# A state-space convolution kernel: the last unit's rows read back step by step, and the last quarter's output made in two halves of 64 channels

## The chip, the cores and the metric

The kernel runs on one core of a Trainium2 chip. A core has a matrix engine (TensorE, in the profile PE, with its weight loads as PEld), VectorE (DVE), ScalarE (ACT), GpSimd (POOL) and SyncE (SP), and sixteen DMA engines that move data between DRAM and the on-chip memory SBUF. TensorE writes its results into another on-chip memory, PSUM. Every engine works through its own list of instructions in order and waits on semaphores. The metric is the time of one execution on the device in microseconds (us), as the median of several runs.

## What is computed

Two diagonal state-space layers (S4 and S4D) are applied to one sequence of 2048 steps and 512 channels. Each is a long causal convolution along the sequence, written with FFTs in the reference, and a gate from a dot product with the input mixes the two results:

```python
def reference(A_u, ..., gate_w):
    x = A_u
    g = _sigmoid((x * gate_w).sum(-1, keepdims=True))
    a = _A_ref(x, ...)   # K = Re sum_n C * exp(dt*A*l) * dt*B;  y = irfft(rfft(u)*rfft(K)) + u*Dskip
    b = _B_ref(x, ...)   # K = 2 Re sum_n C*dt * exp(dt*A*l);    y = irfft(rfft(u)*rfft(K)) + u*D_skip
    return g * a + (1 - g) * b
```

All data are 32-bit floats.

## The kernel before

The 512 channels are worked in eight units of 64, `v` = 0 to 7; two units make a quarter `q` = `v // 2`, which is also the unit of output. For each unit GpSimd, ScalarE, VectorE and TensorE first make the two convolution filters ("tables", `chunk`), TensorE does a first transform stage (`put`), and then `stage2` runs eight steps, `mg` = 0 to 7, over four frequencies each: a forward transform on TensorE (`forward`, line 719), a product with the spectrum `U` of the input on VectorE (lines 791 and 794), an inverse transform on TensorE (lines 803 and 804) into a PSUM bank `hb`, a copy on ScalarE into one of two SBUF buffers `st` (line 807), and a store of 256 KB into the DRAM scratch `wt` (line 810). The spectra `U` are read back from DRAM scratch (line 782); they were stored there earlier in pairs of 128 and 64 partitions (lines 758 to 766).

The last transform needs the data turned: what lay along partitions has to lie in rows. That is what the trip through `wt` is for. `final(q)` reads both units of a quarter back (line 825) and works on four banks `bk`: for each bank two loads of 512 KB, one of unit 2q and one of unit 2q+1, each over 128 partitions, then 16 matmuls with 128 moving columns (64 channels of each unit, line 836) with the weights `wb` and `wg`, which hold the gate, one copy of the bank (line 845 or 847) and one store of 256 KB to the output (line 848). In the last quarter the four banks' rows go into the SBUF buffers `F`, `AB`, `AB` and `Fp` (the last one is a part of the tile `X`, and stands as X in the profile).

The order of all work is made ahead of time, in Python, by a list scheduler (`Plan.run`). Every operation has an engine, an assumed cost, a due time and dependencies. At each point of the modelled time each engine takes, among the operations that are ready and find a free buffer, the one with the lowest due time. DMAs are issued on SyncE's queue; there the model adds 1.1 us and the bytes at 360 GB/s on a single wire, and what depends on a DMA becomes ready 1.2 us after its modelled end. The order that results is emitted as it is: on each engine, SyncE's queue too, an instruction that waits holds up all behind it.

`FILL` names places in TensorE's order (counted in operations) at which spare matmuls of an identity matrix go in (line 300), whose results nobody reads. Place 304 is the first operation of the last quarter's `final`; there 29 units stand ahead of it.

Of the kernel before, what the change touches and what calls it, by code (L numbers as in the profile page):

```python
# [13 lines left out]
P = 128  # L14
L = 2048
D = 512
NJ, NS = 32, 64
NV = 8
EV = (58, 57, 196, 105, 4, 199, 64, 66)
EU = (15, 96, 247, 5)  # L20
NQ = 4
NCH = 128
NCK = 16
CHUNKS = ((1, 0), (1, 1), (0, 0), (0, 1), (1, 2), (1, 3), (0, 2), (0, 3))
LAST = ("Fp", "AB", "AB", "F")
ZU = (95, 116, 87, 62)
GE = 0
OE = (7, 10, 2, 0)
# [34 lines left out]
FPRE = 4.308  # L63
# [11 lines left out]
FW = -2.217  # L75


FILL = {1: 2, 3: 7, 5: 14, 17: 3, 49: 8, 50: 2, 51: 5, 54: 2, 55: 1, 88: 2, 160: 29, 161: 14, 162: 5, 199: 10, 201: 12, 213: 1, 275: 6, 304: 29, 22: 3, 32: 2, 33: 1, 52: 1, 53: 1, 57: 1, 58: 3, 66: 1, 68: 1, 71: 1, 181: 1, 189: 3, 196: 1, 198: 9, 200: 2, 202: 3, 244: 1, 249: 1}


def _flat(t):
# [27 lines left out]
class Plan:  # L109
# [44 lines left out]
    def run(self):  # L154
        free = {t: [(0.0, i) for i in range(len(l))] for t, l in self.tiles.items()}
        caps = {c: [0.0] * n for c, n in CAPS.items()}
        at = dict.fromkeys(("T", "A", "V", "G", "D"), 0.0)
        wire, lanes = 0.0, [0.0] * 8
        table = "E"
        ready = {e: [] for e in at}  # L160
        for o in self.ops:
            o.wait, o.succ = len(o.deps), []
        for o in self.ops:
            for d in o.deps:
                d.succ.append(o)
            if not o.wait:
                ready[o.eng].append((0.0, o))
        n, now, order, turn = 0, 0.0, [], 0
        while n < len(self.ops):
            nxt = 1e30  # L170
            for e in at:
                if at[e] > now:
                    nxt = min(nxt, at[e])
                    continue
                best = None
                for k, (rt, o) in enumerate(ready[e]):
                    if rt > now:
                        nxt = min(nxt, rt)
                        continue
                    key = o.due + (SWITCH if o.func and o.func != table else 0.0)  # L180
                    if best is not None and key >= best[0]:
                        continue
                    need, ok = {}, True
                    for b in o.bufs:
                        if b.slot is None and b.tag:
                            need[b.tag] = need.get(b.tag, 0) + 1
                            if b.cls:
                                need[b.cls] = need.get(b.cls, 0) + 1
                    for t, m in need.items():
                        l = sorted(caps[t]) if t in caps else sorted(f for f, _ in free[t])  # L190
                        if len(l) < m or l[m - 1] > now:
                            ok = False
                            if len(l) >= m:
                                nxt = min(nxt, l[m - 1])
                    if e == "D" and lanes[0] > now:
                        ok = False
                        nxt = min(nxt, lanes[0])
                    if ok:
                        best = (key, k, o)
                if best is None:  # L200
                    continue
                o = best[2]
                ready[e].pop(best[1])
                if e == "T":
                    if turn in FILL:
                        order.append(self.spare(FILL[turn], min((f, t, i) for t in ("ps", "sd") for f, i in free[t])))
                    turn += 1
                cost = o.cost
                if o.func and o.func != table:
                    table, cost = o.func, cost + 1.3  # L210
                at[e] = now + cost
                o.start, o.end = now, now + cost
                if e == "D":
                    wire = max(wire, now + cost + 0.6) + o.nbytes / 360e3
                    o.end = wire
                    lanes = sorted(lanes[1:] + [o.end])
                nxt = min(nxt, at[e])
                for b in o.bufs:
                    if b.slot is None and b.tag:
                        l = free[b.tag]  # L220
                        i = min(range(len(l)), key=lambda j: l[j])
                        b.slot = l.pop(i)[1]
                        b.t = self.tiles[b.tag][b.slot]
                        if b.cls:
                            caps[b.cls].remove(min(caps[b.cls]))
# [20 lines left out]
def gated_s4_mix(ctx: ExitStack, tc: tile.TileContext, ins: dict, out: bass.AP):  # L246
    nc = tc.nc
    V, G, A, T = nc.vector, nc.gpsimd, nc.scalar, nc.tensor
    DMA = nc.sync.dma_start
# [3 lines left out]
    ps = ctx.enter_context(tc.tile_pool(name="ps", bufs=1, space=bass.MemoryType.PSUM))  # L253
    dr = ctx.enter_context(tc.tile_pool(name="dr", bufs=1, space=bass.MemoryType.DRAM))
    pl = Plan()
    op = pl.op
# [9 lines left out]
    wt_t = dr.tile([NV, NJ, P, P], F32, tag="wt", name="wt")  # L266
# [4 lines left out]
    def bank(cls="fb"):  # L271
        return Buf("ps", cls)
# [495 lines left out]
    def both(a):  # L768

        return bass.AP(a.tensor, a.offset, [[512, P], [64 * 512, 2], [1, 512]])  # L770

    def stage2(v, due, sp):
        F, q = Ft[v], v // 2
        fw = [done[v, 0, 0]]
        for mg in range(8):
# [22 lines left out]
            def mms(mg=mg, Z1=Z1, Z2=Z2, hb=hb):  # L798
# [5 lines left out]
                    T.matmul(o, Tw[:, m, 64:192], zv(Z2), start=False, stop=True)  # L804

            op("T", 1.79, dm, mms, r=[Z1, Z2, TwB], w=[hb])
            op("A", 0.48, dm, lambda hb=hb, st=st: A.copy(st.t, hb.t), r=[hb], w=[st])  # L807
            op(
                "D", 0.5, dm,
# [2 lines left out]
                ),  # L812
                r=[st], w=[(wt[v], ((mg, mg + 1),))], nbytes=262144,
            )

    def final(q, due):

        for bk in range(4):
            dy = due + YSP[q] * bk / 4
            f, y, o = Buf(LAST[bk] if q == NQ - 1 else "Fp"), bank(), Buf("st")  # L820
            fv = lambda f=f: f.v("p (u s k c) -> p u s k c", u=2, s=8, k=2, c=64)
            for u in range(2):
                op(
                    "D", 0.5, dy - FPRE,
                    lambda f=f, u=u, bk=bk: DMA(
                        f.v("p (u s c) -> p u s c", u=2, s=8, c=P)[:, u],
                        wt_t[2 * q + u].rearrange("m (x s) c -> (m x) s c", x=4)[:, 8 * bk : 8 * bk + 8],
                    ),
                    r=[wt[2 * q + u]], w=[(f, ((u, u + 1),))], nbytes=524288, after=wdone,
                )  # L830

            def mms(y=y, fv=fv, bk=bk):
                for a in range(4):
                    for k, w in enumerate((wb.t.rearrange("p (s c) -> p s c", c=64), wg)):
                        for e in range(2):
                            T.matmul(  # L836
                                y.t[64 * e : 64 * e + 64, 128 * a : 128 * a + 128].rearrange("p (u c) -> p u c", u=2),
                                w[:, 8 * bk + 4 * e + a, :],
                                fv()[:, :, 4 * e + a, k],
                                start=(k == 0), stop=(k == 1),  # L840
                            )

            op("T", 1.9, dy, mms, r=[f, wgB], w=[y], hold=[wb])
            if OE[q] >> bk & 1:
                op("V", 0.61, dy, lambda o=o, y=y: V.tensor_copy(o.t, y.t), r=[y], w=[o])
            else:
                op("A", 0.48, dy, lambda o=o, y=y: A.copy(o.t, y.t), r=[y], w=[o])
            op("D", 0.5, dy, lambda o=o, bk=bk: DMA(out[q, bk], o.t), r=[o], nbytes=262144)

    wb, wdone = Buf("W"), []  # L850

# [75 lines left out]
    for v in range(NV):  # L927
        if v + 1 < NV:
            tables(v + 1)
        stage2(v, v + 1 + LAG[v], FSP[v])  # L930
        if v % 2:
            final(v // 2, v + 1 + LAG[v] + FSP[v] + FL[v // 2])
    order = pl.run()
    with tc.manual_schedule():
# [115 lines left out]
```

## Time and profile before

| | |
|---|---|
| median of 3 runs | 500.5 us (498.42 to 500.87) |
| the profiled execution | 499.39 us, of which the span from the first to the last instruction is 497.6 us |
| busy share: PE, DVE, ACT, POOL | 90%, 80%, 78%, 79% |
| DMA over the whole span | 85.46 MB, mean 172 GB/s |
| `wt` stores (line 810), 64 of 256 KB | issue to landing 2.9 us (median) |
| the last quarter's matmuls (line 836), from 486.74 us | 7.22 us |

A row of the order in time has the start in us from the span's start, the length in us, the engine, the line, the operation, destination and source by the program's names, the count, and in brackets the idle time of the engine before it and what ended that. SPq is SyncE's DMA queue; the length there is the time that the issuing took, not the transfer. A row of windows has for each stretch the busy time of the five engines with their instructions, then the clock granted to TensorE as a share of full speed, the busy share of the DMA engines (it can pass 1 a little where a transfer reaches past the window's end) and the GB/s moved.

### The profile page before, as it was taken

Reading aid. Unit: us, or ns where it says so; the run is one execution under the profiler, and the core shown is the slowest. Engines: PE = TensorE matmul, PEld = TensorE weight load, DVE = VectorE, ACT = ScalarE, POOL = GpSimd, SP = SyncE. Lnnn points to the kernel's source line nnn. Section 1 sums busy time; section 2 is a strip of 40 time slices with the busy share of each in tenths; the row PEclk is TensorE's granted clock in tenths of the full one; section 3 lists DMA queues with packets and bytes.
Section 4 is the critical chain, followed back from the end, with each engine's and each line's share of the span. In section 5 each row is a group of like instructions: output and inputs, shape, how many; then the busy total and the mean of one; then the engine's idle time right before and its main releaser. Section 6 shows DMA issues by size and latency. Waiting matters only on the chain.

```text
span 497.6 us, 22093 instructions
## 1 busy us (share of the span) xinstructions
PE 449.3 (90%) x9718; PEld 386.4 (78%) x9718; DVE 396.6 (80%) x564; ACT 389.2 (78%) x598; POOL 394.3 (79%) x365
## 2 busy tenths in 40 slices
PE   4798897789999999999989998897999899999996
PEld 3497795678777788888568987487998799889975
DVE  5778797999939888999869988887979999884420
ACT  4679888989999887789999888786999977762111
POOL 4586986989979979999899999688979999950000
PEclk9999999999999999999999999999999999999999
DMA  8969755354554454443308676257245145863846
GB/s 278 397 195 282 218 162 157 102 167 119 157 172 141 132 178 142 127 118 119 107 4 253 184 237 237 50 199 222 67 149 177 62 130 169 268 205 108 302 141 234
DMA packets 69439, 85.46 MB, mean 172 GB/s; under 512 B 4704, under 2 KB 50144, under 8 KB 69088
## 3 DMA queue, kind: packets, MB, share of 16 engines
q1 hardware_dynamic: 69344, 84.06, 53.7%
q8 instruction: 76, 1.25, 1.1%
q14 instruction: 19, 0.16, 0.1%
HBM read 50.49 MB, written 33.59 MB: 169 GB/s over the span
## 4 chain that ended last, share of the span: by engine, by line
PE 41%; ACT 18%; DMA 16%; issue 8%; POOL 8%; DVE 8%; SPq 1%; DVEq 0%; ACTq 0%; POOLq 0%
PE ps L719 8%; PE ps L653 7%; PE ps L803 7%; PE ps L804 6%; PE ps L836 5%; PE ps L696 4%; DMA wt<-st 4%; DMA AB<-in_prm 3%; DMA c_g<-in_c_g 3%; ACT sd L614 3%; DMA X<-wt 3%; POOL E L602 2%; ACT x L615 2%; ACT sd L616 2%; DVE E L632 2%
## 5 line engine op out<-in xcount | busy, mean ns | idle before, releaser
L602 POOL TENSOR_TENSOR E<-AB 128x1024 f32<-128x1024 f32 x64 | 125.3, 1959 | 0.1
L803 PE MATMUL ps<-z,c_t 128*128 128x128 f32 x512 | 102.5, 282 | 3.7 <-DVE z L794 1.8
L804 PE MATMUL ps<-z,c_t 128*128 128x128 f32 x512 | 99.9, 277 | 0.9 <-DVE z L794 0.7
L622 DVE TENSOR_TENSOR QD<-sd,E 128x1024 f32<-128x1024 f32 x64 | 77.9, 1218 | 22.2 <-issue 7.6
L719 PE MATMUL ps<-F,c_g 128*128 128x128 f32 x640 | 83.9, 278 | 1.9 <-ACT F L708 1.2
L803 PEld LDWEIGHTS ps<-z,c_t 128*128 128x128 f32 x512 | 77.6, 191 | 8.9 <-DVE z L794 3.4
L719 PEld LDWEIGHTS ps<-F,c_g 128*128 128x128 f32 x640 | 76.2, 189 | 6.5 <-ACT F L708 1.8
L804 PEld LDWEIGHTS ps<-z,c_t 128*128 128x128 f32 x512 | 77.7, 192 | 2.6 <-DVE z L794 2.5
L632 DVE TENSOR_TENSOR E<-sd,E 128x1024 f32<-128x1024 f32 x64 | 77.8, 1215 | 0.8 <-ACT sd L616 0.8
L583 POOL TENSOR_TENSOR x<-pi,c_tm 128x512 int32<-128x512 int32 x64 | 68.0, 1064 | 11.0 <-ACT sd L616 10.1
L594 POOL TENSOR_TENSOR E<-AB 128x512 f32<-128x512 f32 x64 | 68.5, 1072 | 6.2 <-issue 2.5
L614 ACT ACTIVATE sd<-x 128x1024 f32<-128x1024 int32 x64 | 65.9, 1029 | 8.9 <-DVE QD L627 6.0
L653 PE MATMUL ps<-E 128*32 128x64 f32 x2048 | 64.7, 222 | 7.6 <-DVE E L632 3.3
L616 ACT ACTIVATE sd<-x 128x1024 f32<-128x1024 f32 x64 | 66.0, 1031 | 4.9 <-PE sd L300 2.2
L615 ACT ACTIVATE x<-x 128x1024 f32<-128x1024 int32 x64 | 67.8, 1060 | 1.3
L574 POOL TENSOR_TENSOR x<-gh 128x512 int32<-128x512 int32 x64 | 68.5, 1070 | 0.2
L807 ACT COPY st<-ps 128x512 f32<-128x512 f32 x64 | 37.6, 587 | 38.5 <-PE ps L804 24.9
L653 PE MATMUL ps<-QD 128*32 128x64 f32 x2048 | 63.5, 219 | 3.2 <-issue 3.2
L653 PEld LDWEIGHTS ps<-E 128*32 128x32 f32 x2048 | 48.2, 109 | 21.0 <-issue 10.5
L791 DVE TENSOR_TENSOR z<-ps,U 128x512 f32<-128x512 f32 x64 | 43.8, 685 | 25.0 <-PE ps L719 21.4
L653 PEld LDWEIGHTS ps<-QD 128*32 128x32 f32 x2048 | 49.9, 110 | 4.6 <-issue 4.6
L794 DVE SCALAR_TENSOR_TENSOR z<-ps,sgn,U 128x512 f32<-128x512 f32 x64 | 47.4, 742 | 0.0
(122 smaller groups left out, 786.1 us busy)
## 6 DMA issues: line engine op xcount, KB each, us to landing
U<-ud SPq DMA_DIRECT2D x32, 512.0 KB, 4.0
wt<-st SPq DMA_DIRECT2D x64, 256.0 KB, 2.9
X<-wt SPq DMA_DIRECT2D x26, 512.0 KB, 5.3
ud<-z SPq DMA_DIRECT2D x32, 256.0 KB, 3.6
U<-in_u SPq DMA_DIRECT2D x16, 256.0 KB, 4.6
ud<-z SPq DMA_DIRECT2D x32, 128.0 KB, 3.5
U<-in_uT SPq DMA_DIRECT2D x16, 256.0 KB, 3.5
out<-st SPq DMA_DIRECT2D x16, 256.0 KB, 5.4
```

What stands on the lines that cost most here:

```text
L574: G.tensor_tensor(xi()[:, :, 1, :].rearrange("n c (a b) -> n c a b", a=4), t[:, :, 0:4].unsqueeze(3).to_broadcast([P, NCK, 4, 8]), t[:, :, ...
L594: G.tensor_tensor(Ev()[:, :, 0, :].rearrange("n c (a b) -> n c a b", a=4), A1()[:, ca, ::-1].unsqueeze(3).to_broadcast([P, NCK, 4, 8]), BB ...
L602: G.tensor_tensor(Ev()[:, :, 1:3, :].rearrange("n c w t -> n c (w t)"), AA()[:, ca].rearrange("n c w a -> n (c w) a").unsqueeze(3).to_broa ...
L614: op("A", 0.96, e, lambda: A.activation(bv(sn), wv(xi()), AF.Sin, scale=SCL), r=[x], w=[sn], func="S")
L615: op("A", 0.96, e, lambda: A.activation(x.t, x.v(dt=I32), AF.Abs), w=[x])
L616: op("A", 0.96, e, lambda: A.activation(bv(cs), wv(qv(x)), AF.Sin, bias=HALF_PI, scale=-SCL), r=[x], w=[cs], func="S")
L622: lambda: V.tensor_tensor(ev(QD)[:, :, 0::2, :], bv(sn).rearrange("n w c t -> n c w t"), Ev()[:, :, 0::2, :], ALU.mult),
L632: lambda: V.tensor_tensor(Ev()[:, :, 0:2, :], bv(cs)[:, 0].unsqueeze(2).to_broadcast([P, NCK, 2, NJ]), Ev()[:, :, 0:2, :], ALU.mult),
L653: T.matmul(K4[32 * b : 32 * b + 32, gg, :], ev(QD if w else E)[:, c, 2, :], ev(QD if w else E)[:, c, 0:2].rearrange("n h t -> n (h t)"), s ...
L719: T.matmul(b.v("p (k m h e) -> p m k h e", k=2, m=4, h=32, e=2)[:, mm], Gw[:, m, :], Fv(F)[:, :, m, :].rearrange("p (k h) e -> p k h e", k=2),
L803: T.matmul(o, Tw[:, m, 0:128], zv(Z1), start=True, stop=False)
L804: T.matmul(o, Tw[:, m, 64:192], zv(Z2), start=False, stop=True)
```

## The change

Only unit 7 and the last quarter change; for the quarters 0 to 2 `final` stays as it was.

- In unit 7 each step of `stage2` also reads its four frequencies back as soon as they are stored: a load of 256 KB into 16 partitions of a new SBUF buffer `ft` (tag `F`), 32 rows of 128 channels, 16 KB, in each of these partitions. It takes its due time from its step.
- `final(3)` becomes `final_last(0)` and `final_last(1)`, one for each unit of the quarter. `final_last(0)` reads unit 6's rows with two loads of 1 MB (into `Fp` and `AB`) in place of four of 512 KB, and its matmuls are placed after all of unit 7's inverse transforms. `final_last(1)` uses `ft`. Each makes 16 matmuls for each bank with 64 moving columns, where there were 16 with 128; ScalarE and VectorE take turns in copying the banks' halves of 256 columns into one buffer `fin`. The four stores of 256 KB follow the second half's copies.
- The due times of both are high (50 and 60; the DMAs of unit 6's rows 4.308 less), so they give way to all other work.
- The 29 spare units at place 304 go. TensorE's operations in `final_last` carry a mark (`nbytes=1`) that leaves them out of the count of places.

```diff
-LAST = ("Fp", "AB", "AB", "F")
-FILL = {..., 275: 6, 304: 29, 22: 3, ...}
+FILL = {..., 275: 6, 22: 3, ...}
...
-                    if turn in FILL:
-                        order.append(self.spare(FILL[turn], min((f, t, i) for t in ("ps", "sd") for f, i in free[t])))
-                    turn += 1
+                    at_ = min(((f, t, i) for t in ("ps", "sd") for f, i in free[t]), default=None)
+                    if turn in FILL and at_ and not o.nbytes:
+                        order.append(self.spare(FILL[turn], at_))
+                    turn += not o.nbytes
...
             op("T", 1.79, dm, mms, r=[Z1, Z2, TwB], w=[hb])
+            turned.setdefault(v, []).append(pl.ops[-1])
...
+            if v == NV - 1:
+                op(
+                    "D", 0.5, dm,
+                    lambda mg=mg: DMA(
+                        ft.t[16 * mg : 16 * mg + 16].rearrange("p (s c) -> p s c", c=P),
+                        wt_t[v, 4 * mg : 4 * mg + 4].rearrange("m (x s) c -> (m x) s c", x=4),
+                    ),
+                    r=[(wt[v], ((mg, mg + 1),))], w=[(ft, ((mg, mg + 1),))], nbytes=262144,
+                )
...
+    def last(y, a0, bk, us, fv):
+
+        n = len(us)
+        for a in range(4):
+            for k, w in enumerate((wb.t.rearrange("p (s c) -> p s c", c=64), wg)):
+                for e in range(2):
+                    o = y.t[64 * e : 64 * e + 64, a0 + 64 * n * a : a0 + 64 * n * a + 64 * n]
+                    T.matmul(
+                        o.rearrange("p (u c) -> p u c", u=n) if n > 1 else o, w[:, 8 * bk + 4 * e + a, :], fv(4 * e + a, k),
+                        start=(k == 0), stop=(k == 1),
+                    )
+
+    fin = Buf("AB")
+
+    def final_last(u, due):
+
+        q = NQ - 1
+        for b2 in range(2):
+            dy = due + 0.1 * b2 / 2
+            if u:
+                f, r0 = ft, 16 * b2
+            else:
+                f, r0 = Buf("AB" if b2 else "Fp"), 0
+                op(
+                    "D", 0.5, dy - FPRE,
+                    lambda f=f, b2=b2: DMA(
+                        f.v("p (s c) -> p s c", s=16, c=P),
+                        wt_t[2 * q].rearrange("m (x s) c -> (m x) s c", x=4)[:, 16 * b2 : 16 * b2 + 16],
+                    ),
+                    r=[wt[2 * q]], w=[f], nbytes=1048576, after=wdone,
+                )
+            y = bank()
+            for i in range(2):
+                bk = 2 * b2 + i
+                fv = lambda s, k, f=f, r0=r0 + 8 * i: f.t[:, P * (r0 + s) + 64 * k : P * (r0 + s) + 64 * k + 64]
+                op(
+                    "T", 1.1, dy, lambda y=y, bk=bk, u=u, i=i, fv=fv: last(y, 256 * i, bk, (u,), fv),
+                    r=[f, wgB], w=[(y, ((i, i + 1),))], hold=[wb], nbytes=1,
+                    after=() if u else turned[NV - 1],
+                )
+                e = V if bk % 2 else A
+                op(
+                    "V" if e is V else "A", 0.35 if e is V else 0.3, dy,
+                    ...
+                )
+                if u:
+                    op("D", 0.5, dy, lambda bk=bk: DMA(out[q, bk], fin.t[:, 512 * bk : 512 * bk + 512]), r=[(fin, ((bk, bk + 1), (0, 2)))], nbytes=262144)
...
-        if v % 2:
+        if v == NV - 1:
+            final_last(0, 50.0)
+            final_last(1, 60.0)
+        elif v % 2:
             final(v // 2, v + 1 + LAG[v] + FSP[v] + FL[v // 2])
```

More of the change, by code (lines that the diff above doesn't have):

```diff
@@ L75 @@
 FW = -2.217
-FILL = {1: 2, 3: 7, 5: 14, 17: 3, 49: 8, 50: 2, 51: 5, 54: 2, 55: 1, 88: 2, 160: 29, 161: 14, 162: 5, 199: 10, 201: 12, 213: 1, 275: 6, 304: 29, 22: 3, 32: 2, 33: 1, 52: 1, 53: 1, 57: 1, 58: 3, 66: 1, 68: 1, 71: 1, 181: 1, 189: 3, 196: 1, 198: 9, 200: 2, 202: 3, 244: 1, 249: 1}
+FILL = {1: 2, 3: 7, 5: 14, 17: 3, 49: 8, 50: 2, 51: 5, 54: 2, 55: 1, 88: 2, 160: 29, 161: 14, 162: 5, 199: 10, 201: 12, 213: 1, 275: 6, 22: 3, 32: 2, 33: 1, 52: 1, 53: 1, 57: 1, 58: 3, 66: 1, 68: 1, 71: 1, 181: 1, 189: 3, 196: 1, 198: 9, 200: 2, 202: 3, 244: 1, 249: 1}
 def _flat(t):
@@ L770, in both @@
         return bass.AP(a.tensor, a.offset, [[512, P], [64 * 512, 2], [1, 512]])
+    turned = {}
     def stage2(v, due, sp):
@@ L814, in stage2 @@
             )
+            if v == NV - 1:
[7 more added lines that the diff above has]
+                )
+    ft = Buf("F")
     def final(q, due):
@@ L819, in final @@
             dy = due + YSP[q] * bk / 4
-            f, y, o = Buf(LAST[bk] if q == NQ - 1 else "Fp"), bank(), Buf("st")
+            f, y, o = Buf("Fp"), bank(), Buf("st")
             fv = lambda f=f: f.v("p (u s k c) -> p u s k c", u=2, s=8, k=2, c=64)
@@ new lines, in gated_s4_mix @@
+    fin = Buf("AB")
[27 more added lines that the diff above has]
+                    "V" if e is V else "A", 0.35 if e is V else 0.3, dy,
+                    lambda y=y, i=i, bk=bk, u=u, f=V.tensor_copy if e is V else A.copy: f(
+                        fin.v("p (b a u c) -> p b a u c", b=4, a=4, u=2, c=64)[:, bk, :, u],
+                        y.t[:, 256 * i : 256 * i + 256].rearrange("p (a c) -> p a c", a=4),
+                    ),
+                    r=[(y, ((i, i + 1),))], w=[(fin, ((bk, bk + 1), (u, u + 1)))],
+                )
+                if u:
+                    op("D", 0.5, dy, lambda bk=bk: DMA(out[q, bk], fin.t[:, 512 * bk : 512 * bk + 512]), r=[(fin, ((bk, bk + 1), (0, 2)))], nbytes=262144)
```

## The prediction

> **What bounds the kernel now.** I read the page first, for the span, then the chain of work that ended last (start us, length us, what) from 460 us on, because the change touches only unit 7 and the last quarter.
>
> ```profile
> span 497.6 us, 22093 instructions
> ```
>
> ```profile
> 462.18 8.66 DMA wt<-st
> ...
> 480.33 2.28 DMA wt<-st
> 482.74 3.86 DMA F<-wt
> 486.60 0.14 issue
> 486.74 7.22 PE ps L836 x128
> 493.99 0.04 issue
> 494.03 0.59 ACT st L847
> ```
>
> The end is a relay. Unit 7's last 256 KB go out to DRAM (2.28 us), come back turned in four loads of 512 KB (the first lands after 3.86 us), TensorE then makes the whole last quarter (7.22 us for 128 instructions, 56.4 ns each), ScalarE evicts the last bank (0.59 us), and from 494.62 us to the end of the span the last store takes 3.0 us. Nothing else runs, so what is cut from or added to this relay is cut from or added to the time.
>
> Then the same stretch in order of time, for SyncE's DMA queue, ScalarE and TensorE (start, length, engine, line, operation).
>
> ```profile
> 460.16 0.33 SPq L825 DMA_DIRECT2D F<-wt  x1
> 460.58 0.86 SPq L825 DMA_DIRECT2D AB<-wt  x2
> 461.49 0.64 SPq L825 DMA_DIRECT2D X<-wt  x1
> 462.18 1.23 SPq L810 DMA_DIRECT2D wt<-st  x2
> 465.57 0.36 SPq L782 DMA_DIRECT2D U<-ud  x1
> ...
> 470.94 0.59 ACT L807 COPY st<-ps 128x512 f32<-128x512 f32 x1 [8.26 <-DMA wt<-st]
> 471.55 9.14 SPq L810 DMA_DIRECT2D wt<-st  x6
> ...
> 471.69 0.59 ACT L807 COPY st<-ps 128x512 f32<-128x512 f32 x1 [0.17 <-DMA wt<-st]
> ...
> 474.38 0.59 ACT L807 COPY st<-ps 128x512 f32<-128x512 f32 x1 [2.10 <-DMA wt<-st]
> ...
> 479.47 6.39 PE L300 MATMUL sd<-c_id 128*128 128x512 f32 x16
> 479.71 0.59 ACT L807 COPY st<-ps 128x512 f32<-128x512 f32 x1 [1.20 <-PE ps L804]
> ```
>
> The reader is to see three things. Unit 6's four loads and one U load lie in front of unit 7's first two stores, which land only at about 470.9 and 471.6 us. With two `st` buffers, ScalarE's third and fourth copies wait for just these landings. And the wait from 480 to 486 us is filled on TensorE by 16 spare matmuls, which exist to keep it busy.
>
> **The change, part by part.**
>
> *Unit 6's rows*: four loads of 512 KB become two of 1 MB. They become ready when unit 6's last store has landed, 2 us before the first store of unit 7 is ready, so their low due time puts nothing in front of them. Bytes are the same. I cost this at nothing; what hides it is that TensorE works on unit 7 meanwhile, and without that cover two issues less would be worth 0.8 us at most.
>
> *Unit 7's rows, step by step*: this is the part that decides. Each of the eight steps gets a load of its own, 256 KB into 16 partitions, 16 KB in each. The four loads of 512 KB over 128 partitions, which began at 482.74 us, go. On SyncE's in-order queue the planner has load k ready when store k has landed; at the same moment the `st` buffer comes free, but store k+2 needs a copy first. So the order is load 0, store 2, load 1, store 3, up to store 7, load 6, load 7. A load waits there for store k, and behind it wait store k+2 and, through `st`, ScalarE's copies. Eight issues at about 0.4 us each are no matter on a queue that does six in 9.14 us. [...]
>
> No transfer before touches 16 partitions of SBUF. The nearest row is the store of the filter spectra, line 758: each pair sends 256 KB from 128 partitions and then 128 KB from 64. Here are the DMA engines from 98 to 104 us in 40 slices, and windows (last two columns: busy share of the engines, GB/s) while the first and the second of a pair ran.
>
> ```profile
> GB/s 0 0 0 0 0 0 102 321 437 328 328 260 191 198 184 150 69 0 7 14 7 68 14 27 20 75 328 355 341 341 321 225 225 177 178 116 0 0 0 0
> ...
> ud<-z SPq DMA_DIRECT2D x3, 256.0 KB, 2.2
> ud<-z SPq DMA_DIRECT2D x3, 128.0 KB, 2.5
> ```
>
> ```profile
> 102.00:102.60 0.60, 0.56 (x6) 0.37 (x5) 0.21 (x1) 0.32 (x1) 0.60 (x2) 1.00 1.01 345
> 102.75:103.20 0.45, 0.45 (x7) 0.45 (x6) 0.45 (x1) 0.00 (x0) 0.45 (x1) 1.00 0.88 205
> ```
>
> Per busy share the rate is 345/1.01 = 342 with 128 partitions and 205/0.88 = 233 GB/s with 64: 0.68 for one halving, and it repeats in the pair before (328, then about 190). From 128 to 16 partitions are three halvings. The bounds: at the full 342 a load of 256 KB holds the engines 0.77 us; if the loss stops at 64 partitions, 233 GB/s, 1.13 us, or 1.4 at the raw 190; with 0.59 (205/345) for each halving, 70 GB/s, 3.7 us; in proportion to the partitions, 43 GB/s, 6.1 us. I take 0.68 three times, 108 GB/s, **2.4 us**, the milder reading of the only row there is.
>
> [...]
>
> Now the engines' queue from the moment when load 0 can go:
>
> ```profile
> 470.90:472.00 1.10, 0.47 (x4) 0.43 (x4) 0.00 (x0) 0.90 (x2) 0.00 (x0) 1.00 0.78 291
> ```
>
> The U load still holds the engines to about 472.0 us. Then come eight loads at 2.4 and six stores at 0.77 us: 19.2 + 4.6 = 23.8 us. They leave no gap, because while load k runs (2.4 us), the copy and the issue of store k+2 (0.59 + 0.1 us, and about 0.9 us to its first byte, my share of the 2.28) are done. So the last byte comes at 495.8, and with some 0.4 us to the semaphore (the rest of the 2.28) the rows are there at **496.2 us instead of 486.60: +9.6**.
>
> *The output in two halves*: each bank's 16 matmuls (32 instructions) of 128 columns become two sets of 16 with 64 columns. The bounds per instruction: half of 56.4, 28 ns; no gain, 56 ns, if loading the 128x64 weights sets the pace, since each half loads them all again. The nearest row is stage 1, where four 64x64 tiles run at a time:
>
> ```profile
> 443.51 1.09 PE ps L696 x64
> ```
>
> 17.0 ns per instruction with 64 columns, so with two tiles at a time 34 ns, 1.09 us per bank and half. I take that: 4.35 us for each half (3.6 to 7.2). The first half, 4.35 us with four evictions, follows unit 7's last matmuls (just ahead of the copy at 479.71 us; an estimated 1.5 us later with ScalarE's copies held up) and lies wholly in the wait. It takes the place of the spare matmuls, which go. The second half replaces 7.22 us: **-2.9**.
>
> *The clock*: TensorE now has nothing from about 485.5 to 496.3 us. Before, such a hole lies only behind the last matmul (493.96 us), and there the granted clock (the column ahead of the DMA share) falls:
>
> ```profile
> 497.60:499.50 1.90, 0.00 (x0) 0.00 (x0) 0.00 (x0) 0.00 (x0) 0.00 (x0) 0.68 0.02 4
> ```
>
> A mean of 0.68 over 1.9 us is 0.68 us at 1 and the rest at a half: a fall at 498.3 us, 4.3 us after the last matmul. So the second half starts slow: between 0 and all of its 4.35 us again; I take the middle, **+2.2**. [...]
>
> *Eviction and store*: the last bank's copy has 256 columns, by 0.59 for 512 about 0.4 us: **-0.2**. The four stores come every 1.09 us, above the 0.77 that one holds the engines, so the last 3.0 us stay.
>
> The sum: 9.6 - 2.9 + 2.2 - 0.2 = **+8.7 us**. The profiled execution took 499.39 us (span 497.6); its 508.1 is my number for the changed kernel, rounded to **508**. The median of the three runs is 500.5, 1.1 above; on it the sum would be 509.2.
>
> **The rivals.**
>
> *The loads run at full speed* (the other side: faster). Place: the engines from 472 us on. It decides below about 1.3 us a load, where the queue of loads and stores is empty before store 7 is ready. For it: with 16 KB rows, as these are, the tables came in at 440 GB/s, though over 128 partitions.
>
> ```profile
> 12.00:16.00 4.00, 3.81 (x68) 2.58 (x68) 3.86 (x6) 4.00 (x14) 1.70 (x3) 1.00 1.03 440
> ```
>
> Against it: the 64-partition windows. Then store 7 lands as before at 482.6, load 7 lands about 2.3 us later, at 485.0 (-1.6), the second half follows warm (-2.9), the eviction (-0.2): -4.7, **494.7**, and 495.8 on the median.
>
> *The loss stops at 64 partitions.* 1.13 to 1.4 us a load: at 1.4 the queue is 8 x 1.4 + 4.6 = 15.8 us from 472.0, rows at 488.2 (+1.6), -2.9, and 2.2 at most for the clock after a hole of 4 us: between -1.5 and +0.7; at 1.13 it is 13.6 us, rows at 486.0: -0.6 - 2.9 - 0.2 = -3.7. Together **495.7 to 500.1**. For it: one halving is all that the trace shows.
>
> *The loss is in proportion to the partitions.* 3.7 to 6.1 us a load add 8 x 1.3 to 8 x 3.7 us to the forecast: **518 to 538**. For it: 0.59 per halving by the raw windows; against it the share-corrected 0.68.
>
> *The halves aren't halves.* If weight loads set the pace, the second half takes 7.2 us, 2.85 more: 511 with slow loads, 497.6 with fast ones; so the change would give almost nothing even without the DMA's cost. Against it: 17 ns in stage 1, whose weights are also reloaded for each 64 columns.
>
> **How the numbers follow.** Slow loads of about 2 to 3 us: 0.66, among them 0.06 with halves that aren't halves. Full speed: 0.14. Stop at 64: 0.11. In proportion: 0.09. About 0.5% (2.5 us) is what can be told from no change here. Faster by more: full speed with halves that are halves (0.13) and some of stop at 64 (0.03), 0.16. Within it: the rest of both but for 0.01, 0.08. Slower: the two slow cases, 0.76 with that hundredth. The forecast's own range is 504 (2.0 us a load) to 514 (3.0 us and the full price of the clock). The stated range goes down to 495.5 to take in stop at 64 and half of full speed, and up to 514; it leaves out the proportional case and the better half of full speed.
>
> **What would show it.** Packets of 16 KB that take far more than at full rate, 100 to 120 GB/s at full DMA share between 472 and 496 us; landing of the loads into F of 4 us and more; ScalarE's copies L807 waiting on stores up to about 485 us; a hole on TensorE of about 10 us ahead of the last 128 instructions, and a granted clock under 1 in them. Wrong would be: loads landing in 2.3 us, the rows there at 485, and a second half at 34 ns right behind the first.

## The result, and the profile after

The changed kernel takes 506.26 us (median of 4 runs, 505.69 to 506.85), the kernel before in the same runs 500.68 us (median of 4, 498.42 to 500.87): a ratio of 1.0116, 95% interval 1.0084 to 1.0149. It is slower, by about 5.6 us. The profiled execution took 506.36 us, before 499.39: +6.97, of which +6.7 lies in the span (504.3 against 497.6).

The page's head and the chain of work that ended last (start us, length us, what), from the third copy of unit 7 on:

```profile
span 504.3 us, 22321 instructions
```

```profile
471.14 0.59 ACT st L810
...
472.76 6.68 DMA wt<-st
...
479.54 0.59 ACT st L810
480.15 4.36 DMA wt<-st
...
485.22 4.84 DMA wt<-st
...
490.07 4.68 DMA F<-wt
...
495.11 5.29 PE ps L871 x128
...
500.42 0.38 ACT AB L907
...
500.82 0.42 DVE AB L907
```

Before, the chain ran from the third copy over TensorE up to the last copy at 479.71 us, and the only DMAs behind it were the last store and one load. Now it is DMA from 472.76 to 494.75 us: stores of 4.4 to 6.7 us where the last one took 2.28 before, and a last load of 4.68 us. The last copy for unit 7 now waits for stores, and so the last store begins at 485.22 instead of 480.33 us.

SyncE's queue in order of time (start, length of the issue, line), and ScalarE's copies with the wait ahead of each:

```profile
471.10 0.34 SPq L821 DMA_DIRECT2D F<-wt  x1
471.75 0.37 SPq L813 DMA_DIRECT2D wt<-st  x1
472.22 0.45 SPq L821 DMA_DIRECT2D F<-wt  x1
472.76 1.43 SPq L813 DMA_DIRECT2D wt<-st  x1
477.19 0.32 SPq L821 DMA_DIRECT2D F<-wt  x1
...
488.34 2.06 SPq L821 DMA_DIRECT2D F<-wt  x2
```

```profile
477.23 0.59 ACT L810 COPY st<-ps 128x512 f32<-128x512 f32 x1 [4.74 <-DMA wt<-st]
...
484.61 0.58 ACT L810 COPY st<-ps 128x512 f32<-128x512 f32 x1 [1.90 <-DMA wt<-st]
```

Load and store alternate from the first one on, and the copies from the fifth on (the fifth and the eighth are shown) wait for a store. The view of line 821 gives the loads' time from issue to landing:

```profile
DMA to landing us min/median/max: 4.2/4.7/6.4
```

Last the windows (PE, PEld, DVE, ACT, POOL busy, then granted clock, DMA share, GB/s): loads and stores together, the last load alone, the time after its last byte, and the second half's matmuls in two parts.

```profile
478.00:484.00 6.00, 5.74 (x94) 5.43 (x96) 0.00 (x0) 1.17 (x2) 0.00 (x0) 1.00 1.14 222
...
490.90:493.50 2.60, 0.00 (x0) 0.00 (x0) 0.00 (x0) 0.00 (x0) 0.00 (x0) 0.56 0.73 101
...
495.10:498.10 3.00, 2.99 (x57) 3.00 (x58) 0.00 (x0) 0.00 (x0) 0.00 (x0) 0.51 0.00 0
498.10:500.20 2.10, 2.10 (x78) 2.10 (x74) 0.42 (x1) 0.37 (x1) 0.00 (x0) 1.00 0.17 65
```

```profile
493.50:494.70 1.20, 0.00 (x0) 0.00 (x0) 0.00 (x0) 0.00 (x0) 0.00 (x0) 0.50 0.01 0
```

The last load, with the engines to itself, moves 101 GB/s. In its first 3.0 us the second half runs at half clock and gets through 57 instructions, 53 ns each; the other 71 take 2.30 us at full clock (498.10 to 500.40), 32 ns each. (A window also counts instructions that reach over its edge, so 57 and 78 are more than 128 together; and it counts a transfer's bytes where its packets start.) The difference of the two spans splits as follows, along the chain:

| piece of the chain | before | after | difference |
|---|---|---|---|
| last matmuls begin (rows there, plus 0.14 and 0.36 us) | 486.74 | 495.11 | +8.37 |
| last matmuls' length | 7.22 | 5.29 | -1.93 |
| from their end to the end of the span | 3.64 | 3.90 | +0.26 |
| sum | | | +6.70 |

### The profile page after: what moved, and what is told of

Same layout as the page of the kernel before. It is cut to its first block, busy times and chain, and to the rows that moved or that the text cites. A ratio compares the mean times of both kernels' runs of the same rounds, so it can differ in the third digit from the quotient of the medians.

```text
span 504.3 us, 22321 instructions
## 1 busy us (share of the span) xinstructions
PE 448.4 (89%) x9830; PEld 387.4 (77%) x9830; DVE 398.5 (79%) x568; ACT 388.0 (77%) x598; POOL 394.2 (78%) x365
## 4 chain that ended last, share of the span: by engine, by line
PE 42%; DMA 19%; ACT 15%; DVE 11%; issue 8%; POOL 4%; SPq 1%; DVEq 0%; ACTq 0%; POOLq 0%
PE ps L719 8%; PE ps L653 8%; PE ps L805 6%; PE ps L806 5%; DMA wt<-st 5%; PE ps L696 5%; DMA c_g<-in_c_g 3%; DMA X<-wt 3%; DMA U<-in_uT 3%; PE ps L850 3%; ACT sd L614 3%; PE ps L931 2%; DVE E L632 2%; DMA AB<-in_prm 2%; ACT x L615 2%
## 5 line engine op out<-in xcount | busy, mean ns | idle before, releaser
L793 DVE TENSOR_TENSOR z<-ps,U 128x512 f32<-128x512 f32 x64 | 43.7, 683 | 26.7 <-PE ps L719 21.7
```

## The experiments

The theory is that of the prediction: a load into 16 neighbouring partitions holds the DMA engines some 2.4 us, eight of them in front of and between the stores make the rows late. The rivals were that the length of the rows does it, the count of partitions or which ones they are, or the mere place of loads between stores. A second question was what the two halves bring by themselves, and what the cold clock costs.

**How the runs are compared.** The order of work ahead of unit 7's stores is the same in all these kernels, but for unit 6's rows, which all the changed ones read in two loads; yet the moment at which unit 7's third copy on ScalarE starts (the one that the first store's landing releases) differs between profiled executions from 467.0 to 479.4 us. So the tail is counted from that copy: 470.94 us before, 471.14 after. "Rows there" is the landing of the last load of unit 7's rows (for the kernel before, e7, e9 and e11 the first of four, with the last in brackets). All differences are of rows of the chain, "end" is the span less the third copy. The expectations of e1 to e4 named spans, and these came out at 497.2, 501.9, 494.6 and 500.0 us, all outside what was named: the start of the tail moves by more than the effects that were looked for. So these runs, one profile each, are read by their tails alone.

| kernel | third copy | last store issued | rows there | last matmuls, us | end |
|---|---|---|---|---|---|
| before | 470.94 | +9.39 | +15.66 (+19.7) | 7.22 | +26.7 |
| after | 471.14 | +14.08 | +23.6 | 5.29 | +33.2 |
| e1, 128 partitions | 471.54 | +11.26 | +18.1 | 3.50 (64 instructions) | +25.7 |
| e2, 16 partitions, 2 KB pieces | 469.24 | +13.45 | +22.9 | 5.42 | +32.7 |
| e3, 32 partitions | 467.03 | +11.68 | +20.1 | 3.26 (64) | +27.6 |
| e4, every 8th of 128 partitions | 470.62 | +11.72 | +19.4 | 5.71 | +29.4 |
| e5, 64 partitions | 473.50 | +11.90 | +19.7 | 3.70 (64) | +27.4 |
| e6, spares in the hole | 478.31 | +13.12 | +22.0 | 3.97 | +30.3 |
| e7, halves, wide loads at the end | 479.36 | +9.47 | +18.0 (+21.9) | 7.51 with two waits | +29.2 |
| e8, loads of two steps | 470.96 | +13.03 | +22.7 | 5.74 | +32.8 |
| e9, e7 warmed, own bank each | 478.55 | +9.59 | +18.1 (+22.1) | 5.30 | +27.2 |
| e10, a repeat | 470.70 | +14.43 | +24.4 | 5.37 | +34.1 |
| e11, e9 with spares before | 470.87 | +9.49 | +15.9 (+22.3) | with waits | +27.4 |
| e12, first half last | 471.17 | +13.66 | +22.2 | 10.40 (256) | +36.7 |

In e1 to e5 unit 7's rows lie at other places of `ft`, so the last transform takes other rows for the 64 channels of unit 7; its work is the same. In e1, e3 and e5 the first two banks need only what steps 0 to 3 brought, so half of the second half was done while the chain still waited: their last matmuls and end can't be set against the others', their loads and stores can.

**e1: the eight loads over all partitions**

```diff
-  ft.t[16 * mg : 16 * mg + 16].rearrange("p (s c) -> p s c", c=P),
-  wt_t[v, 4 * mg : 4 * mg + 4].rearrange("m (x s) c -> (m x) s c", x=4),
+  ft.t[:, 512 * mg : 512 * mg + 512].rearrange("p (s c) -> p s c", c=P),
+  wt_t[v, 4 * mg : 4 * mg + 4].rearrange("m (x s) c -> (m x) s c", x=32),
```

> Each step's load brings the same 256 KB into 128 partitions, 2 KB in each, in place of 16 partitions with 16 KB; the rows then lie in other places, so the 64 channels of unit 7 are not the reference's. [...] If it is the traffic itself (a load between two stores, or reading what was just written), loads still take 4 to 5 us and the span stays within 502 to 505.

The end of its chain:

```profile
482.80 3.92 DMA wt<-st
...
486.74 2.87 DMA F<-wt
...
489.74 3.50 PE ps L871 x64
```

The rows are there 18.1 us after the third copy, 5.5 us sooner than in the change. So the width of the loads matters. But the eight loads still take 2.8 to 4.2 us to land, where the rival of full speed had 2.3, and the rows come 2.4 us later than the first rows of before, and 4.0 later than the 14.1 us (485.0 - 470.94) of the rival "the loads run at full speed". Its windows show the traffic:

```profile
472.00:478.00 6.00, 5.08 (x43) 4.72 (x42) 2.60 (x4) 1.69 (x4) 0.00 (x0) 1.00 0.85 237
478.00:484.00 6.00, 6.00 (x137) 5.88 (x138) 0.42 (x1) 1.73 (x4) 0.00 (x0) 1.00 1.01 252
```

Loads and stores together move 237 to 252 GB/s even at full width, and eight loads and six stores of 256 KB (3.67 MB) take 14.6 us at 252. The step-by-step loads put 2 MB among the stores that before came after them.

**e2: the same 16 partitions, but pieces of 2 KB in place of 16 KB rows**

```diff
-  ft.t[16 * mg : 16 * mg + 16].rearrange("p (s c) -> p s c", c=P),
+  ft.t[16 * mg : 16 * mg + 16].rearrange("p (j w) -> p j w", w=512),
```

> Still 16 partitions, but each is filled with eight separate pieces of 2 KB in place of one run of 16 KB (the pieces come from other places, so unit 7's 64 channels are not the reference's). Few partitions as the cost: loads land in 4 to 5 us as before, span 503 to 506. Long rows, one for each DMA engine, as the cost: 2.3 to 3 us and a span of 493 to 496.

```profile
482.69 4.92 DMA wt<-st
...
487.63 4.51 DMA F<-wt
```

Rows at +22.9 us: as in the change, whose repeats (after, e6, e10, e12) lie between +22.0 and +24.4. The length of the rows is not the cause.

**e3, e5, e4: 32 partitions, 64 partitions, and 16 that are spread**

```diff
+  ft.t[32 * (mg % 4) : 32 * (mg % 4) + 32, 2048 * (mg // 4) : 2048 * (mg // 4) + 2048]     (e3)
+  ft.t[64 * (mg % 2) : 64 * (mg % 2) + 64, 1024 * (mg // 2) : 1024 * (mg // 2) + 1024]     (e5)
+  ft.t[mg : mg + 121 : 8]                                                                  (e4)
```

> The same 256 KB for each step into 32 partitions with 8 KB each (other places, unit 7's 64 channels not the reference's). [...] If the traffic itself is the cost, 502 to 505.

> The 256 KB of each step into 64 partitions with 4 KB each (other places, unit 7's 64 channels not the reference's). The runs start their tails up to 4 us apart, so I count from the third copy of unit 7 on ScalarE; from there the last rows landed after 23.6 us in the change (16 neighbours), 20.1 with 32, 19.4 with every 8th, 18.1 with 128. [...] If each halving of the count costs, 64 stands between 32 and 128: 18.7 to 19.2 us.

> Step k's sixteen rows of 16 KB go to partitions k, k+8, k+16 and so on to k+120, in place of sixteen neighbours (contracted with other weights, so unit 7's 64 channels are not the reference's). Count of partitions and length of rows are as in the change. By count or by row length nothing changes: loads land in 4 to 5 us, span 503 to 506. [...]

The last store and load of e4, where each load goes into 16 partitions that lie 8 apart:

```profile
482.34 4.22 DMA wt<-st
...
486.57 3.40 DMA F<-wt
```

```profile
487.80:489.20 1.40, 0.00 (x0) 0.00 (x0) 0.00 (x0) 0.00 (x0) 0.00 (x0) 0.50 0.77 187
```

e4 has the same 16 partitions in number and the same 16 KB in each as the change, and its rows are there at +19.4 us, with those of 32 (+20.1) and 64 partitions (+19.7), and not with those of 16 neighbours (+22.0 at the least). Its last load, with the engines to itself (the window), moves 187 GB/s, where the change's moves 101. So it is not the count of partitions but where they lie: 19.4 to 20.1 us for 32 neighbours, 64 neighbours and every eighth partition, 22.0 to 24.4 for 16 neighbours. What it is about their place that decides, no run shows. (The 18.1 us of 128 partitions is sooner than both, but by 1.3 us only and in one profile, while profiles of the change's own loads differ by 2.4 us; that step is not shown.)

**e6: the change with 36 units of spare matmuls in the hole, the time in which TensorE waits for the rows**

```diff
+                    if o.due == 60.0 and not warmed:
+                        order.append(self.spare(36, at_))
+                        warmed = True
```

> The change with 36 spare matmuls of the identity (about 8 us of TensorE) between the first and the second half. If the clock that fell in the hole is what makes the second half's first 56 instructions take 53 ns each, all 128 take 29 ns: 3.75 us in place of 5.29, and from the third copy to the end it takes 31.6 us in place of 33.2. If the slow start has another cause (the first use of the buffer, say), nothing changes.

```profile
496.28 4.02 DMA F<-wt
...
500.65 3.97 PE ps L875 x128
```

```profile
500.60:504.60 4.00, 3.95 (x128) 3.84 (x128) 0.42 (x1) 0.37 (x1) 0.00 (x0) 1.00 0.14 51
```

At a clock of 1.00 the second half takes 3.97 us for 128 instructions, 31 ns each. Against 5.29 in the change the cold clock costs 1.3 us. (The rows were 1.6 us sooner after the third copy too, which the spares don't explain; it lies in the spread of the repeats.)

**e7, e9 and e11: the halves without the loads step by step.** Here unit 7's rows come as before, four loads of 512 KB over 128 partitions behind the last store, and only the division into halves is left of the change. e9 adds twelve units of spares in the hole and a PSUM bank for each bank of the second half; e11 adds eight units ahead of the first half.

```diff
-            if v == NV - 1:
-                op("D", 0.5, dm, lambda mg=mg: DMA(ft.t[16 * mg : 16 * mg + 16]..., ...), ...)
...
+                for bk in (2 * b2, 2 * b2 + 1):
+                    op("D", 0.5, dy - FPRE, lambda bk=bk: DMA(ft.t[:, 1024 * bk : 1024 * bk + 1024]..., ...),
+                        r=[wt[NV - 1]], w=[(ft, ((bk, bk + 1),))], nbytes=524288)
...
+                    if o.due == 60.0 and not warmed:                                          (e9)
+                        order.append(self.spare(12, at_))
...
+                if u:
+                    y = bank()
...
+                    if o.due in (50.0, 60.0) and o.due not in warmed:                         (e11)
+                        order.append(self.spare(8 if o.due == 50.0 else 12, at_))
```

> The second part of the change alone: two halves, but unit 7's rows come back after the last store in four loads of 512 KB over 128 partitions, one for each bank, as before the change. From the third copy the first load lands after 15.7 us and the last after 19.7 us as before, the second half follows the loads, and the end comes after about 24.7 us where the kernel before has 26.7: 2 us faster, 0.4%. If the halves bring nothing, 26.7.

e7: ratio 1.0044, interval 1.0005 to 1.0083. The last store is issued 9.47 us after the third copy, as before (9.39): the delay of 4.7 us that the change has there comes from its loads alone. But the halves bring nothing; the end, expected at +24.7 us, came at +29.2. The end of the chain:

```profile
488.83 4.23 DMA wt<-st
...
497.48 1.99 PE ps L862 x32
...
499.55 0.38 ACT AB L907
...
499.97 3.40 PE ps L862 x64
...
503.39 0.38 ACT AB L907
...
503.81 1.18 PE ps L862 x32
```

The last store, issued in time, lands only after 4.23 us where before's took 2.28, and the first of the last rows are there at +18.0 us in place of +15.66; e9 shows the same. Then the first 32 instructions run cold (62 ns each), and twice TensorE stops for the copy of a bank that the next matmuls write again.

> The halves alone with wide loads after the last store, as in the run before, with two mends: 12 spare matmuls (2.6 us) in TensorE's hole, and a PSUM bank of its own for each bank of the second half, so that no bank's matmuls wait for the copy of the one before. If the cold clock and those waits ate the gain, the end comes 24 to 25 us after the third copy and the kernel is 0.3 to 0.5% faster than before the change. If the wide loads alone set the end (the last lands 19.7 us after the third copy whatever TensorE does), no more than 1.3 us, 0.25%, can be won. If neither, a ratio of 1.00 or above.

e9: ratio 0.997, interval 0.9931 to 1.001, no difference that can be told; the end was at +27.2 us, not at 24 to 25. (In the profiled executions of e7 and e9, which took 510.67 and 507.55 us, the third copy came some 8 us later than before's; only what follows that copy is read here.) The twelve units did not keep the clock up: it was 0.54 from 496.70 to 500.00 us. The last store, issued in time, lands late: 4.15 us. The DMA view from 488 to 493 us, in 40 slices, shows in it a transfer on another queue, q8, of 16 KB of instructions:

```profile
GB/s 287 287 283 119 0 0 0 0 135 295 291 295 274 295 279 189 21 12 131 0 0 0 0 0 0 8 4 0 0 0 0 0 0 0 0 0 0 0 0 0
...
q8 instruction: 1, 0.02, 1.2%
...
wt<-st SPq DMA_DIRECT2D x1, 256.0 KB, 4.1
```

The fetch is the 131 at 490.25 us. By then the store is through but for some 1.5 KB, which follow as 8 and 4 at about 491.3 us. So its last packets come about 1.1 us later, behind the fetch; why the landing takes another 0.9 us, to 492.28, the view doesn't show. In e7 too a transfer on q8 falls into the last store, at 491.07 us.

The kernel before has no such transfer between 480.3 and 482.7 us, and its store lands in 2.3 us:

```profile
q1 hardware_dynamic: 587, 0.28, 38.4%
...
wt<-st SPq DMA_DIRECT2D x1, 256.0 KB, 2.3
```

> e9 with eight spare matmuls more, ahead of the first half, so that the fetch of instructions that fell into the last store in e9 falls elsewhere. If the fetch is what holds the last store: its landing falls from 4.15 us to about 2.3, the first of the last rows land about 16.2 us after the third copy instead of 18.08, the end comes 24.5 to 25.5 us after it (e9 27.15, before 26.7), and the ratio to the kernel before is 0.990 to 0.996. If something else holds it (the four 512 KB loads that come behind it): the store still lands in 4.1 to 4.4 us, the end 27 us after the third copy, ratio 0.997 or above.

e11 moves that fetch by adding instructions ahead of it. Its chain, and the landings of its four loads:

```profile
480.36 2.28 DMA wt<-st
...
484.70 7.24 DMA F<-wt
```

```profile
DMA to landing us min/median/max: 3.9/7.0/8.0
```

The store is back at 2.28 us, and the first of the last rows are there at +15.9 us (482.90, the first load's issue, and its 3.9): so far the expectation held. The rest of it did not: ratio 1.002, interval 0.9985 to 1.0054, the end at +27.4 us in place of 24.5 to 25.5. The fetch now falls into the loads. The DMA view from 482.8 to 492 us:

```profile
q8 instruction: 1, 0.02, 0.6%
...
F<-wt SPq DMA_DIRECT2D x4, 512.0 KB, 7.0
```

The loads of before took 3.9, 5.3 and 6.6 us (shortest, median, longest), those of e9 4.1, 5.5 and 6.8; there a fetch starts only as the last bytes go (490.07 and 500.06 us, 0.6 us ahead of the last landing). Those of e11, with a fetch at their start (483.4 us), took 3.9, 7.0 and 8.0. So a fetch goes together with the slow transfer in all three kernels: with the store in e7 and e9, with the loads in e11. In e11 it is not shown to be the cause: from 485 to 489 us, when the fetch of under 1 us is over, the loads move 270 GB/s, where before moved 377 in the same window.

**e8: half as many loads, each of two steps**, 512 KB into 32 partitions after every second store.

```diff
-            if v == NV - 1:
+            if v == NV - 1 and mg % 2:
-                        ft.t[16 * mg : 16 * mg + 16].rearrange("p (s c) -> p s c", c=P),
+                        ft.t[16 * mg - 16 : 16 * mg + 16].rearrange("p (s c) -> p s c", c=P),
```

> The change with one load for every two steps, 512 KB into 32 neighbouring partitions, which holds the engines as long as one load of the change does: half the time in all. [...]

No gain: ratio 1.0108, interval 1.0073 to 1.0143, the change over again.

```profile
483.99 4.89 DMA wt<-st
...
488.93 4.75 DMA F<-wt
...
493.81 5.74 PE ps L871 x128
```

The last load has twice the bytes of the change's and takes as long (4.75 against 4.68 us). But the last copy still waits for a store that went with a load, and the last store itself, with a load issued just ahead of it, lands in 4.89 us:

```profile
483.38 0.58 ACT L810 COPY st<-ps 128x512 f32<-128x512 f32 x1 [4.24 <-DMA wt<-st]
```

The expectation looked at the engines' time alone. Here the end hangs on landings that follow one another: store, copy, last store (+13.03 us), and behind it a load twice as large.

**e10 and e12: is the first half hidden?** e10 gave the first half's matmuls a dependency on unit 7's rows in the planner; e12 puts them behind the second half's in TensorE's own order.

```diff
-                    r=[f, wgB], w=[(y, ((i, i + 1),))], hold=[wb], nbytes=1,                  (e10)
+                    r=[f, wgB] + ([] if u else [ft]), w=[(y, ((i, i + 1),))], hold=[wb], nbytes=1,
...
-                    after=() if u else turned[NV - 1],                                        (e12)
+                    after=() if u else late,
...
-            final_last(0, 50.0)
-            final_last(1, 60.0)
+            final_last(1, 50.0)
+            final_last(0, 60.0)
```

> The change with its loads step by step, but the first half too waits for the last rows, so that TensorE has both halves to do at the end. If the halves are worth what they hide, the end moves from 33.2 us after the third copy to about 37 (3.75 us more, less what the loads vary from run to run), with only the first 3 us at half clock. If the first half was not on the way to the end in any case, 33.

e10 tells nothing on the question: the order on TensorE stayed as it was, so the first half did not wait, and the last 128 instructions took 5.37 us as in the change. It serves as a repeat: end at +34.1 us against +33.2, so two profiles of the same work differ by 0.9 us in the tail.

> The change, with the matmuls of the first half put behind those of the second in TensorE's own order, so that both follow the last rows. If the first half was hidden in the wait (measured 3.75 us of it in the change, 485.9 at the latest, rows at 494.76): the end comes 33.2 + 3.75 = about 37 us after the third copy. If the wait for the rows covers less of it than that, or the order of the two halves does not matter: 33 to 34.5 us, as in the change.

```profile
493.54 10.40 PE ps L871 x256
```

```profile
497.00:500.00 3.00, 3.00 (x69) 3.00 (x67) 0.42 (x1) 0.37 (x1) 0.00 (x0) 0.58 0.00 0
```

With both halves behind the rows TensorE needs 10.40 us, 5.1 more than in the change, and the end comes at +36.7 us, where about 37 was expected. So the first half is hidden in the change. That the number fits is partly luck: this run's rows were 1.4 us sooner, so at equal rows hiding the first half is worth about 4.9 us (36.7 and 1.4, less 33.2). Some 1.2 us of the 5.1 are the clock: a mean of 0.58 from 497.00 to 500.00 us puts its rise at 499.5 us, 6.0 us into the work, where it rose after 3.0 us in the change. The rest, 3.9 us, is the first half itself (482.16 to 486.11 us in the change).

## Why the prediction was right, point by point

The number was 508.1 us for the profiled execution; it took 506.36. The mechanism held: the eight loads held the engines, the stores and through them ScalarE's copies came late, and the shorter last matmuls did not pay for it. The terms:

| term | predicted | measured |
|---|---|---|
| rows there | +9.6 (496.2) | +8.15 (490.07 + 4.68 = 494.75, less 486.60) |
| second half, warm | -2.9 (4.35 us) | -3.25 (3.97 us, e6) |
| cold clock | +2.2 | +1.3 (5.29 against 3.97) |
| copies and last store | -0.2 | +0.26 |
| rows there to first matmul | none | +0.22 (0.36 against 0.14) |
| sum | +8.7 | +6.7 |

- **The load's price** was right: 2.4 us was taken from three halvings of 0.68, 2.6 us is what 256 KB need at the 101 GB/s of the last load. The way to it was lucky, though. The loss does not go by halvings of the count: the rows of e3, e4 and e5 are there at about the same time, from 64 partitions down to 16 spread ones, with 187 GB/s for e4's last load, and the further loss comes only for 16 neighbours. That the loss stops at 64 partitions, as one rival had it, is true of 32 neighbours and of spread places, not of these 16.
- **The sum over the queue was the term that was mis-sized.** It put eight loads and six stores one behind the other, 19.2 + 4.6 = 23.8 us from 472.0. The last byte came at 493.5 us (no bytes behind it in the window from there on), 21.5 us for eight loads, 2.7 each. That they go strictly one after the other, as this sum takes it, no run shows: the stores' 4.6 us went almost wholly into the loads' time; in the window from 478 to 484 us 222 GB/s flow (180 from 472.0 to 493.6) where a load alone moves 101. On the other hand 1.25 us passed from the last byte to the landing (494.75), where 0.4 was put. The two make 495.8 into 493.5, and 496.2 into 494.75.
- **The full-speed rival was priced wrong**, though it was not the case that happened. It had 2.3 us for the last load's landing and no delay of the stores; e1 has 2.87, and its last store 1.9 us late (+11.26 against +9.39). Loads between the stores cost 2.4 us against before's first rows even at full width.
- **The halves are halves**: 31 ns per instruction with 64 columns in e6, where 34 were taken and 56 was the other bound. That e7, e9 and e11 still gain nothing was not among the rivals: in e9 the second half was shorter on TensorE (5.30 us against 7.22), but the last store took 1.9 us longer; in e11 the loads took longer; in e7 the store took longer and TensorE, with its waits, was no shorter (7.51).
- **The cold clock**: it fell as forecast, in the window from 490.90 to 493.50 us (a mean of 0.56 is full speed for the first 0.3 us, so the fall is at 491.2; the first half's last matmul ended at 486.1, so it came after 5.1 us, where 4.3 were put; before, the views of 497.60 to 498.30 and of 498.30 to 499.50 us give 0.98 and 0.50), and stood at half when the rows came (0.50 from 493.50 to 494.70). It stayed so for 3.0 us (0.51 from 495.10 to 498.10), in which 57 instructions were done that need 1.8 us at e6's 31 ns. So the price was 1.2 to 1.3 us, less than the 2.2 from the middle of the bounds. But the stretch is not the same in all runs: it was about 3.9 us in e4 (0.51 from 490.30 to 494.30) and e8 (0.50 from 493.80 to 497.80) and 6.0 us in e12, where by the same working the price is some 2.5 us. So neither 1.3 nor 2.2 is a size to rely on.
- **The eviction**: the last bank's two halves of 256 columns go to ScalarE and VectorE, but VectorE's copy starts (500.82) when ScalarE's of the same PSUM bank has ended. From the last matmul to the last copy it is 0.84 us (500.40 to 501.24) where the single copy of 512 columns had 0.66 (493.96 to 494.62), so the term has the other sign. ScalarE's copy of the bank's first half (500.42), too, starts only behind the bank's last matmul, so the copies come in two pairs (498.61 and 499.01, 500.42 and 500.82) and not one every 1.09 us. The view gives ScalarE's copy as what VectorE's waited for; whether the chip or the order that the program sets demands it was not tried.
- **Unit 6's rows as two loads** cost nothing that can be seen (the first store behind them lands after 8.72 us, before 8.66), and the order load 0, store 2, load 1, store 3 was as forecast.
- **Three details were read wrongly**, with no effect on the sum. Line 758 stores the spectra of the input, not of the filters. The tables that came in at 440 GB/s had rows of about 24 KB (1.76 MB in 72 packets from 12 to 16 us), not 16 KB. And the ends of the forecast's own range are, by its own terms, 504.9 (2.0 us a load) and 515.0 (3.0 us and the full price of the clock), not 504 and 514.

What stays open: what about the place of 16 partitions makes a load into them slow; why the rows of kernels with the same loads come at +22.0 in one profile and at +24.4 in another (a fetch of instructions falls into the last store of both, e6 and e10, and not into that of e12 with +22.2); how much of the late last store in e7 and e9 is the fetch of instructions, and what slows the loads of e11; and what the halves alone could bring if no fetch fell between the last store and the last rows, since no such version was run. No version that was run beats the kernel before by more than can be told.

## What to carry to other kernels

Before a transfer is cut up and moved forward, price it at the place where it will run: here small loads into 16 neighbouring partitions held the DMA engines 2.6 us for 256 KB, and put between the stores of a chain they delayed the last store that the chain waits for from +9.39 to +14.08 us. Where a load must go into 16 partitions, look at which ones: here every eighth one was as fast as 64 in a row (rows at +19.4 and +19.7 us). And look at the granted clock behind a wait that work on TensorE hides: here that work ended 9.0 us before the rows were used, and the first 3.0 us of what followed ran at 0.51; with 36 units of spares in the wait (e6) it ran at 1.00.

## What the runs showed of the hardware that was not expected

- Sixteen partitions lying 8 apart take a 256 KB load as well as 32 or 64 neighbours (rows at +19.4, +20.1 and +19.7 us), 16 neighbours don't (+22.0 to +24.4). Alone, such a load moved 187 GB/s spread (e4) and 101 into neighbours.
- Stores from SBUF ran beside loads into few partitions almost for nothing: 222 GB/s together where such a load alone has 101; at full width both together reached 252 (e1).
- A fetch of 16 KB of instructions on a queue of its own went together with a last store of 4.2 us in place of 2.3 (e7, e9); the store's last packets came behind the fetch. With more instructions ahead of it (e11) the fetch fell elsewhere, and the store took 2.28 us.
- After a hole the granted clock stayed at half for 3.0 us of new work in the change, about 3.9 in e4 and e8 and 6.0 in e12.
- Copies of two halves of one PSUM bank on ScalarE and VectorE did not run at the same time in this kernel's end: 0.38 and 0.42 us, one after the other.
